# Moving a routing table's one-hot rows to GpSimd, and the first row transposes into the last AV

## Chip, cores and metric

One core of one Trainium2 chip. The time is the device time of one execution in microseconds; the kernel before has a median of 217.82 us over 14 runs (214.29 to 222.69).

## What is computed

Causal attention over 4 batches, 8 heads, 768 positions and a head dimension of 64, in which heads 0, 2 and 6 see the whole past and the others see only 4 sink positions and a window of 64. Its output, as 3072 token rows of 512 elements, goes through a mixture of experts: token n belongs to expert `domain_id[n]`, one of 8.

```python
mask = np.where(retr[0, :, 0, 0, None, None], full_mask, stream_mask)   # per head
a = softmax(np.where(mask, scale * q @ k.T, -1e9))
x = (a @ v).transpose(0, 2, 1, 3).reshape(B * S, H * D)                 # 3072 x 512
for e in range(E):                                                       # 8 experts
    mask = domain_id == e
    h = np.maximum(x[mask] @ w1[e], 0.0)                                 # 512 -> 1024
    out[mask] = h @ w2[e]                                                # 1024 -> 512
```

## The kernel before

The program is written in one order by hand, and each engine works through its own instructions in that order. It has three parts.

**Attention.** 16 pairs of heads, four to a batch: (0, 2), (6, 7), (1, 3), (4, 5). A loop over n = 0 to 16 does the scores of pair n and the AV product of pair n - 1. In pass n, `hooks(n)` issues on the SP queue the loads of q, k and v of pair n + 4, and on GpSimd the casts to fp16: q and k of pair n + 2 (`cast_qk`, L155), v of pair n + 1 (`cast_v`, L175). The fp32 q and k tiles have 3 buffers each, the fp32 v tiles 4, the fp16 q and k tiles 2. So the load of q for pair n + 3 needs pair n's cast, and the cast of pair n + 2 needs pair n's transposes. TensorE transposes q and k (L302), VectorE or ScalarE copies them out of PSUM (L311), TensorE makes the scores (L338, with mask matmuls L321), ScalarE the exponentials (L349), TensorE the AV product (L391), and VectorE normalises (L403, L404) into `xb`. `store_x(b)` (L417) writes a batch's rows to a table `x_tok` in DRAM.

A pass has one to three steps, by the pair's kind: 3 for (0, 2), 2 for (6, 7), 1 for the other two. Behind step x of pass n stand the pieces of the routing that a table names for (n, x).

**Routing.** `routing_items` makes, from the domain ids, the slot of each token: one-hot of the experts (`one_hot`), counts ahead of each partition by three small matmuls (`ranks`), a running count (`scan`), the own rank (`own`), the slot number `dst` (`place`, `place2`), its low 7 bits `lof` and its high part `hif` (`split`). Then the slot table is turned round by a matmul: for each of the 24 token columns, a one-hot row of the low part over 128 (`low`, L577, tiles `ohl`) and of the high part over 28 (`high`, L555; `high2` L563 and `high3` L571 multiply it by the column and by the partition number, tile `ohh`). `rows` multiplies them by 24 matmuls (L588) and starts the conversion on VectorE, `rows2` and `rows3` finish it: `out_i`, and the row numbers `map_i` (all batches) and `map_e` (the first three batches only). `flags` sets a flag for a slow path that is not taken here. All arithmetic of the routing is VectorE's.

**MoE.** Experts are handled in pairs, in groups of 128 slots. `load_w` (L194 for w1, L201 for w2) loads and converts weights; `load_xe` (L661) gathers rows of `x_tok` by `map_e` or `map_i` by indirect DMAs. All these are issued on GpSimd's queue. Of pairs 0 and 1, groups 0, 1, 3 and 4 hold tokens of the first three batches in their first 256 slots of an expert ("early" gathers, issued from `hooks(14)`); groups 2, 6 and 5 ("late") need batch 3 as well and follow `store_x(3)`. `x_transpose` (L683) turns rows, VectorE copies them (L696, L690), `layer1` (L711, L718) and `layer2` (L761, L775) follow, and the results leave by indirect DMAs (L727).

In the last pass, n = 16, there are no scores. TensorE is given dummy matmuls on a zero tile (`keep_warm`, L842): four ahead of the last AV and eight behind it, and after these the first row transposes.

```python
if n == NPAIR:
    av0 = [lambda: keep_warm(4, "exp")] + av0
    av1 = av1 + [lambda: keep_warm(8, "last"), lambda: x_transpose(0, 0, 1, wide=True)]
```

Of the kernel before, what the change touches and what calls it, by code (L numbers as in the profile page):

```python
# [9 lines left out]
FP16 = mybir.dt.float16  # L10
FP32 = mybir.dt.float32
# [10 lines left out]
def kernel(  # L22
# [125 lines left out]
            )  # L148
            q32_t[nm, n] = t

    def cast_qk(n, engs=None):
        for x, nm in enumerate("qk"):
            t = tpool.tile([P, NSO, 2, D], FP16, tag=f"{nm}16", name=f"{nm}_{n}")
            eng = engs[x] if engs else nc.gpsimd
            eng.tensor_copy(  # L155
                out=t[:].rearrange("p t h d -> p h t d"), in_=q32_t[nm, n][:]
            )
            qk_t[nm, n] = t
# [32 lines left out]
    def load_w(e, which):  # L191
        if which == 1:
            t = wpool.tile([P, 2, 2, F], FP16, tag="w1", name=f"w1_{e}")
            nc.gpsimd.dma_start(  # L194
                out=t[:].rearrange("p c r f -> p c (r f)"),
                in_=moe_w1[e].rearrange("(c p r) f -> p c (r f)", p=P, r=2),
            )
        else:
            tag = "w2" if e < 6 else "w1"
            t = wpool.tile([P, 2, 4, DM], FP16, tag=tag, name=f"w2_{e}")  # L200
            nc.gpsimd.dma_start(  # L201
                out=t[:].rearrange("p c r d -> p c (r d)"),
                in_=moe_w2[e].rearrange("(c p r) d -> p c (r d)", p=P, r=4),
            )
        w_t[e, which] = t
# [210 lines left out]
    def store_x(b):  # L416
        nc.sync.dma_start(  # L417
            out=x_d[1 + b * S : 1 + (b + 1) * S, :].rearrange("(p t) d -> p t d", p=P), in_=xb[b][:]
        )


    def routing_items():
        V = nc.vector
        R = {}

        def tile_(shape, dtype, name):
            R[name] = rpool.tile(shape, dtype, name=name)
            return R[name]
# [13 lines left out]
        dest_i = tile_([P, NT], I32, "dest_i")  # L442
        lo = tile_([P, NT], I32, "lo")
        hi = tile_([P, NT], I32, "hi")
        lof = tile_([P, NT], FP16, "lof")
        hif = tile_([P, NT], FP32, "hif")
        fl = tile_([1, 2], FP32, "fl")
        ohl = [
# [55 lines left out]
        def place():  # L504
            V.tensor_scalar(out=odd[:], in0=dom32, scalar1=1, scalar2=None, op0=ALU.bitwise_and)
            V.scalar_tensor_tensor(
                out=dst[:], in0=dom32, scalar=float(CAP), in1=rank[:], op0=ALU.mult, op1=ALU.add
            )
            V.scalar_tensor_tensor(
                out=dst[:], in0=odd[:], scalar=float(MAIN - CAP), in1=dst[:],  # L510
                op0=ALU.mult, op1=ALU.add,
            )
            V.tensor_scalar(
                out=ta[:], in0=odd[:], scalar1=float(HALF - MAIN), scalar2=float(MAIN),
                op0=ALU.mult, op1=ALU.add,
            )
            V.scalar_tensor_tensor(
                out=ta[:], in0=rank[:], scalar=float(MAIN + 1), in1=ta[:],
                op0=ALU.is_ge, op1=ALU.mult,
            )  # L520
# [39 lines left out]
            )  # L560

        def high2():
            V.tensor_tensor(  # L563
                out=ohh[:, :, 1, :],
                in0=ohh[:, :, 0, :],
                in1=c32[:, CF_T : CF_T + NT].unsqueeze(2).to_broadcast([P, NT, NHI]),
                op=ALU.mult,
            )

        def high3():  # L570
            V.tensor_scalar(  # L571
                out=ohh[:, :, 0, :], in0=ohh[:, :, 0, :], scalar1=c32[:, CF_P : CF_P + 1],
                scalar2=None, op0=ALU.mult,
            )

        def low(t):
            V.tensor_tensor(  # L577
                out=ohl[t // 12][:, t % 12 : t % 12 + 4, :],
                in0=c16[:, C_IO : C_IO + P].unsqueeze(1).to_broadcast([P, 4, P]),
                in1=lof[:, t : t + 4].unsqueeze(2).to_broadcast([P, 4, P]),  # L580
                op=ALU.is_equal,
            )

        def rows():
            t_ = ps_s.tile([P, 1024], FP32, tag="sp", name="map_ps")
# [31 lines left out]
        def rows3():  # L617
# [19 lines left out]

        lows = [lambda t=t: low(t) for t in range(0, NT, 4)]
        return {
            (1, 0): (one_hot,), (1, 1): (ranks,), (2, 0): (scan,), (3, 0): (own,),  # L640
            (4, 0): (place,), (4, 1): (place2,), (4, 2): (split,), (5, 0): (high,),
            (6, 0): (high2,), (7, 0): (high3,), (8, 0): lows[0:1], (8, 1): lows[1:2],
            (8, 2): lows[2:3], (9, 0): lows[3:4], (9, 1): lows[4:5], (10, 0): lows[5:6],
            (11, 0): (rows,), (12, 0): (rows2,), (12, 1): (rows3,), (12, 2): (flags,),
        }

    xe_t, xT_t, hT_t = {}, {}, {}
# [24 lines left out]
    def x_transpose(pr, *gs, wide=False):  # L672
        for e in (2 * pr, 2 * pr + 1):
            if e not in xT_t:
                xT_t[e] = mpool.tile([P, 4, CAP], FP16, tag="xT", bufs=4, name=f"xT_{e}")
        if wide:
            ps = ps_s.tile([P, 4, 4, P], FP16, tag="sp", name=f"xtp_{pr}_{gs[0]}")
        else:
            ps = ps_b.tile([P, 2, 4, P], FP16, tag="b", name=f"xtp_{pr}_{gs[0]}")
        for x, g in enumerate(gs):  # L680
            for c in range(4):
                c1, r = divmod(c, 2)
                nc.tensor.transpose(  # L683
                    out=ps[:, x, c, :],
                    in_=xe_of(pr, g)[:, c1 * 256 + r : (c1 + 1) * 256 : 2],
                    identity=id_sb,
                )
        if gs[0] == 6:
            for i in range(2):
                nc.vector.tensor_copy(  # L690
                    out=xT_t[2 * pr + i][:, :, MAIN:CAP],
                    in_=ps[:, 0, :, i * HALF : (i + 1) * HALF],
                )
        else:
            e, o, n = 2 * pr + gs[0] // 3, (gs[0] % 3) * P, len(gs)
            nc.vector.tensor_copy(  # L696
                out=xT_t[e][:, :, o : o + n * P].rearrange("p c (g k) -> p c g k", g=n),
                in_=ps[:, 0:n].rearrange("p g c k -> p c g k"),
            )
# [110 lines left out]
    def hooks(n):  # L810
        b, pi = divmod(n, 4)
        if n == 4:
            for r in range(VR):
                load_vs(r, 1)
        if n + 4 < NPAIR:
            load_qk(n + 4)
            load_v((n + 4) // 4, (n + 4) % 4)
        if n + 2 < NPAIR:
            cast_qk(n + 2)
        if n == 14:  # L820
            for g in (0, 1):
                load_xe(0, g, 3)
        if n + 1 < NPAIR:
            cast_v((n + 1) // 4, (n + 1) % 4)
        if n == 13:
            load_w(0, 1)
        if n == 14:
            load_w(1, 1)
            for g in (3, 4):
                load_xe(0, g, 3)  # L830
            load_w(2, 1)
            for g in (0, 1):
                load_xe(1, g, 3)
            load_w(3, 1)
            for g in (3, 4):
                load_xe(1, g, 3)

    def keep_warm(m, tag):
        pool, tag_, cols = (ps_b, "b", 512) if tag in (0, 1) else (ps_s, "sp", 1024)
        ps = pool.tile([P, cols], FP32, tag=tag_, name=f"warm_{tag}")  # L840
        for _ in range(m):
            nc.tensor.matmul(  # L842
                out=ps[:, 0:DM], lhsT=zrow[:, 0:P], rhs=zrow[:], start=True, stop=True
            )
# [8 lines left out]
    for n in range(NPAIR + 1):  # L853
        if n < NPAIR:
            hooks(n)
        R = len(plans[n % 4]) // 2 if n < NPAIR else 1
        av0, av1 = av_items(n - 1) if n >= 1 else ([], [])
        tr = []
        if n == NPAIR:
            av0 = [lambda: keep_warm(4, "exp")] + av0  # L860
            av1 = av1 + [lambda: keep_warm(8, "last"), lambda: x_transpose(0, 0, 1, wide=True)]
        elif n + 1 < NPAIR:
            q_evac = nc.scalar.copy if R == 1 else nc.vector.tensor_copy
            tr = [lambda: transposes(n + 1, q_evac, R == 1)]
        if R == 1:
            run(tr)
        if n == 0:
            av0 = [lambda: keep_warm(3, 0)]
        steps = {1: [av0 + av1], 2: [tr, av0 + av1], 3: [av0 + av1, tr, []]}[R]
        for x, step in enumerate(steps):  # L870
            if n < NPAIR:
                scores(n, (2 * x, 2 * x + 1))
            run(step)
            if x == 0 and n % 4 == 0 and 0 < n < NPAIR:
                store_x(n // 4 - 1)
            for fn in route.get((n, x), ()):
                fn()
    store_x(B - 1)
    load_w(0, 2)
    for g in (2, 6, 5):  # L880
        load_xe(0, g)
    for g in (2, 6, 5):
        load_xe(1, g)
    load_w(1, 2)
    for g in range(4):
        load_xe(2, g)
# [159 lines left out]
```

## Time and profile before

| what | value |
|---|---|
| median of 14 runs | 217.82 us |
| the profiled execution's own time | 218.66 us |
| its span, first to last instruction | 216.9 us |
| TensorE busy | 187.6 us (86%) |
| VectorE busy | 95.2 us (44%) |
| ScalarE busy | 90.0 us (41%) |
| GpSimd busy | 118.9 us (55%) |
| granted TensorE clock, mean | 0.936 |
| chain that ended last, largest parts | TensorE 70%, DMA 11%, GpSimd 6%, VectorE 5% |

The profile names each instruction by its line in the kernel (L155 is line 155). PE is TensorE's matmuls, PEld its weight loads, DVE VectorE, ACT ScalarE, POOL GpSimd, SP the queue that loads q, k and v. A timeline row has the start and the duration in us, and in brackets the idle time of the engine before it with what ended that. The chain of waits is followed back from the last instruction, at each step to what released it. Busy shares are means over the whole span; what a piece of work costs is read from its own stretch.

### The profile page before, as it was taken

The page shows a single profiled execution, that of the slowest core. Times are in us where ns is not written, and L with a number is a line of the kernel's source. Part 1 is how long each engine was busy: PE and PEld are TensorE (multiplying, and loading weights), DVE is VectorE, ACT ScalarE, POOL GpSimd, SP SyncE. Part 2 cuts the span into 40 slices and gives each one's busy share as a digit, 9 for nine tenths or more (in the row PEclk, how much of TensorE's full clock was granted, in tenths as well). Part 3 has the DMA queues.
Part 4 walks back from the last instruction along what each step waited for, and adds up shares of the span by engine and source line. Part 5 has one row for each costly group of instructions (what it writes and reads, how often), then busy time and mean ns, then how long its engine had stood idle before and what let it go on. Part 6 is the DMA issues. An engine that isn't in the chain of part 4 may idle for free.

```text
span 216.9 us, 5471 instructions
## 1 busy us (share of the span) xinstructions
PE 187.6 (86%) x2295; PEld 124.5 (57%) x2295; DVE 95.2 (44%) x200; ACT 90.0 (41%) x115; POOL 118.9 (55%) x154
## 2 busy tenths in 40 slices
PE   7687795999899798889957899999999999999920
PEld 2345663787587366569955895555554555444510
DVE  4337689867998965331201204440045200444310
ACT  2474585658887755306523571006600165000000
POOL 7815778644757667700578712657837600550670
PEclk9799999579999969789996999999999999999985
DMA  6999999999999899999949999997899999961241
GB/s 194 284 286 303 303 278 272 342 324 299 314 328 274 277 165 216 238 235 275 217 119 179 259 193 214 257 165 246 146 186 259 239 217 243 259 214 51 105 158 65
DMA packets 44448, 49.87 MB, mean 230 GB/s; under 512 B 28799, under 2 KB 37248, under 8 KB 44418
## 3 DMA queue, kind: packets, MB, share of 16 engines
q0 software_dynamic: 9472, 26.80, 55.2%
q1 hardware_dynamic: 34802, 22.60, 37.5%
q8 instruction: 20, 0.33, 0.6%
q10 hardware_dynamic: 144, 0.07, 0.2%
q14 instruction: 10, 0.08, 0.1%
HBM read 56.83 MB, written 10.49 MB: 310 GB/s over the span
## 4 chain that ended last, share of the span: by engine, by line
PE 70%; DMA 11%; POOL 6%; DVE 5%; issue 3%; ACT 2%; SPq 1%; POOLq 1%
PE h L711 23%; PE o L761 18%; DMA k<-in_k_dram 11%; PE av L391 8%; PE sp L338 5%; PE xtp L683 4%; PE o2h L775 3%; POOL k L155 2%; PE sp L321 2%; PE tp L302 1%; POOL out_dram L727 1%; DVE kT L311 1%; POOL ve L175 1%; ACT eT L349 1%; SPq L145 1%
## 5 line engine op out<-in xcount | busy, mean ns | idle before, releaser
L349 ACT ACTIVATE eT<-sp 128x1024 f16<-128x1024 f32 (+2 forms) x56 | 50.2, 953 | 19.4 <-PE sp L338 19.4
L718 ACT ACTIVATE hT<-h 128x512 f16<-128x512 f32 (+2 forms) x48 | 31.8, 668 | 61.2 <-PE h L711 58.6
L711 PE MATMUL h<-xT,w 128*128 128x256 f16 (+2 forms) x384 | 51.7, 293 | 5.3 <-issue 1.9
L727 POOL DMA_INDIRECT out_dram<-oute,out_i x27 | 27.2, 1006 | 42.6 <-DVE oute L725 31.0
L711 PEld LDWEIGHTS <-w 128*128 128x128 f16 x384 | 39.2, 114 | 16.3 <-issue 4.5
L761 PE MATMUL o<-w,hT 128*128 128x512 f16 x184 | 41.9, 379 | 0.0
L725 DVE COPY oute<-o 128x512 f32<-128x512 f32 x23 | 15.9, 692 | 51.6 <-PE o L761 48.9
L761 PEld LDWEIGHTS <-hT 128*128 128x128 f16 x184 | 17.5, 98 | 19.8 <-issue 0.8
L338 PE MATMUL sp<-qT,kT 64*64 64x128 f16 (+8 forms) x468 | 22.6, 255 | 5.1 <-DVE kT L311 3.7
L661 POOL DMA_INDIRECT xe<-x_tok,map_i x16 | 16.3, 1018 | 16.6 <-SPq L950 12.1
L391 PEld LDWEIGHTS <-eT 128*128 128x128 f16 (+2 forms) x672 | 21.8, 104 | 6.2 <-issue 3.2
L391 PE MATMUL av<-ve,eT 128*128 128x65 f16 (+2 forms) x572 | 23.6, 199 | 1.0 <-POOL ve L175 0.7
L155 POOL CAST q<-q 128x768 f16<-128x768 f32 x15 | 12.9, 857 | 18.5 <-DMA q<-in_q_dram 12.3
L696 DVE COPY xT<-xtp 128x1024 f16<-128x1024 f16 (+1 forms) x16 | 8.9, 553 | 26.4 <-PE xtp L683 22.9
L338 PEld LDWEIGHTS <-kT 64*64 64x64 f16 (+2 forms) x468 | 11.7, 105 | 12.5 <-issue 4.4
L404 DVE TENSOR_TENSOR xb<-av,rcp 128x384 f16<-128x384 f32 x32 | 17.8, 558 | 1.1
L321 PE MATMUL sp<-c16s 128*128 128x128 f16 (+2 forms) x152 | 15.7, 297 | 2.2 <-ACT eT L349 1.9
L175 POOL CAST ve<-v 128x384 f16<-128x384 f32 x32 | 17.2, 565 | 0.0
L155 POOL CAST k<-k 128x768 f16<-128x768 f32 x15 | 12.8, 854 | 5.8 <-DMA k<-in_k_dram 5.1
L321 PEld LDWEIGHTS <-c16s 128*128 128x128 f16 (+1 forms) x152 | 7.7, 107 | 6.8 <-issue 5.8
L403 DVE RECIPROCAL rcp<-av 128x6 f32<-128x6 f32 x32 | 6.1, 192 | 11.5 <-PE av L391 11.5
L661 POOL DMA_INDIRECT xe<-x_tok,map_e x8 | 8.3, 1043 | 4.7 <-DVE fl L549 1.9
(96 smaller groups left out, 169.9 us busy)
## 6 DMA issues: line engine op xcount, KB each, us to landing
w<-in_moe_w_dram POOLq DMA_DIRECT2D x16, 1024.0 KB
q<-in_q_dram SPq DMA_DIRECT2D x16, 384.0 KB, 6.3
k<-in_k_dram SPq DMA_DIRECT2D x16, 384.0 KB, 5.9
v<-in_v_dram SPq DMA_DIRECT2D x32, 192.0 KB, 5.8
x_tok<-xb SPq DMA_DIRECT2D x4, 768.0 KB, 6.4
out_dram<-oute,out_i POOLq DMA_INDIRECT x27
c16s<-c SPq DMA_DIRECT2D x1, 320.5 KB, 6.2
xe<-x_tok,map_i POOLq DMA_INDIRECT x16
```

The lines of the kernel that those rows point to most:

```text
L155: eng.tensor_copy(out=t[:].rearrange("p t h d -> p h t d"), in_=q32_t[nm, n][:])
L175: nc.gpsimd.tensor_copy(out=ve_t[b][:, :, h, 0:D], in_=v_t[b, pi][:, hh])
L321: nc.tensor.matmul(out=sp[o, c : c + w], lhsT=c16[rows, C_ID + rows.start : C_ID + rows.stop], rhs=c16[rows, col : col + w], start=(c // 5 ...
L338: nc.tensor.matmul(out=sp[o : o + m, c : c + w], lhsT=kT[n][rows, k0 : k0 + m], rhs=qT[n][rows, i0 : i0 + w], start=False, stop=True, skip ...
L349: nc.scalar.activation(out=eT[n, r // 3][:, r % 3, c0:c1], in_=sp[:, c0:c1], func=AF.Exp, scale=scale)
L391: nc.tensor.matmul(out=ps[m0 : m0 + m, it, :], lhsT=eT[n, r // 3][rows, r % 3, c : c + m], rhs=rhs, start=(cell["n"] == 1), stop=(cell["n" ...
L404: nc.vector.tensor_tensor(out=xb[b][:, :, h * D : (h + 1) * D], in0=ps[:, :, 0:D], in1=rcp[:].unsqueeze(2).to_broadcast([P, NSO, D]), op=A ...
L661: nc.gpsimd.indirect_dma_start(out=xe_of(pr, g), out_offset=None, in_=x_d[0 : 1 + nb * S, :], in_offset=bass.IndirectOffsetOnAxis(ap=(map_ ...
L711: nc.tensor.matmul(out=pv[:, a, c0:c1], lhsT=w_t[e, 1][:, c // 2, c % 2, fc * 512 + fr : (fc + 1) * 512 : 4], rhs=xT_t[e][:, c, c0:c1], st ...
L718: nc.scalar.activation(out=hT_t[e][:, 2 * f2 : 2 * f2 + 2, c0:c1], in_=pv[:, :, c0:c1], func=AF.Relu)
L727: inst = nc.gpsimd.indirect_dma_start(out=out, out_offset=bass.IndirectOffsetOnAxis(ap=out_i[:, s : s + 1], axis=0), in_=o[:], in_offset=None,
L761: nc.tensor.matmul(out=ps[:], lhsT=hT_t[e][:, f, g * P : (g + 1) * P], rhs=w_t[e, 2][:, f // 4, f % 4, :], start=(f == 0), stop=(f == 7),)
```

## The change

It has five parts.

1. The 24 one-hot rows of the low part go from six VectorE instructions of 4 x 128 elements to 24 GpSimd instructions of 128 (a comparison with a scalar that is read per partition; `lof` becomes fp32 for that). The products `high2` and `high3` go to GpSimd as well; `high` stays on VectorE.
2. The table that places the routing's pieces is rewritten: the count, scan and rank pieces come one step or so earlier, the rest of `place` (now `place1`), `place2` and `split` stand together behind step (4, 2), the one-hot rows at (5, 0), (5, 1), (8, 0) to (8, 2) and (9, 0), `rows` at (12, 0) in place of (11, 0), and `rows2`, `rows3` at (12, 1) and (12, 2).
3. The load of expert 0's w1, which stood behind the v cast of pair 14, is issued between the q and k casts of pair 15.
4. Both groups of dummy matmuls in the last pass go, and the first row transposes stand in the middle of the last AV's first half.
5. Behind the last store, the six late gathers are issued ahead of the load of expert 0's w2.

In the order of GpSimd's instructions the compares come in three groups: eight between the v cast of pair 6 and the q cast of pair 8, twelve between the v cast of pair 9 and the q cast of pair 11, four and then `high2` between the v cast of pair 10 and the q cast of pair 12; `high3` follows the v cast of pair 11. Ahead of the first compare the built program has one instruction more than before, a reload of GpSimd's instruction library.

```diff
-    def cast_qk(n, engs=None):
+    def cast_qk(n, engs=None, between=None):
         for x, nm in enumerate("qk"):
+            if x and between:
+                between()
...
-        lof = tile_([P, NT], FP16, "lof")
+        lof = tile_([P, NT], FP32, "lof")
...
                 out=dst[:], in0=odd[:], scalar=float(MAIN - CAP), in1=dst[:],
                 op0=ALU.mult, op1=ALU.add,
             )
+
+        def place1():
...
         def high2():
-            V.tensor_tensor(
+            G.tensor_tensor(
...
         def high3():
-            V.tensor_scalar(
+            G.tensor_scalar(
...
         def low(t):
-            V.tensor_tensor(
-                out=ohl[t // 12][:, t % 12 : t % 12 + 4, :],
-                in0=c16[:, C_IO : C_IO + P].unsqueeze(1).to_broadcast([P, 4, P]),
-                in1=lof[:, t : t + 4].unsqueeze(2).to_broadcast([P, 4, P]),
-                op=ALU.is_equal,
-            )
+            for u in range(t, t + 4):
+                G.tensor_scalar(
+                    out=ohl[u // 12][:, u % 12, :], in0=c16[:, C_IO : C_IO + P],
+                    scalar1=lof[:, u : u + 1], scalar2=None, op0=ALU.is_equal,
+                )
...
-            (1, 0): (one_hot,), (1, 1): (ranks,), (2, 0): (scan,), (3, 0): (own,),
-            (4, 0): (place,), (4, 1): (place2,), (4, 2): (split,), (5, 0): (high,),
-            (6, 0): (high2,), (7, 0): (high3,), (8, 0): lows[0:1], (8, 1): lows[1:2],
-            (8, 2): lows[2:3], (9, 0): lows[3:4], (9, 1): lows[4:5], (10, 0): lows[5:6],
-            (11, 0): (rows,), (12, 0): (rows2,), (12, 1): (rows3,), (12, 2): (flags,),
+            (0, 2): (one_hot,), (1, 0): (ranks,), (1, 1): (scan,), (2, 0): (own,),
+            (3, 0): (place,), (4, 2): (place1, place2, split), (5, 0): lows[0:1],
+            (5, 1): lows[1:2], (8, 0): lows[2:3], (8, 1): lows[3:4], (8, 2): (lows[4], high),
+            (9, 0): lows[5:6], (9, 1): (high2,), (10, 0): (high3,),
+            (12, 0): (rows,), (12, 1): (rows2,), (12, 2): (rows3,), (13, 1): (flags,),
...
-            cast_qk(n + 2)
+            cast_qk(n + 2, between=lambda: load_w(0, 1) if n == 13 else None)
...
-        if n == 13:
-            load_w(0, 1)
...
         if n == NPAIR:
-            av0 = [lambda: keep_warm(4, "exp")] + av0
-            av1 = av1 + [lambda: keep_warm(8, "last"), lambda: x_transpose(0, 0, 1, wide=True)]
+            k = len(av0) // 2
+            av0 = av0[:k] + [lambda: x_transpose(0, 0, 1, wide=True)] + av0[k:]
...
     store_x(B - 1)
+    for pr in range(2):
+        for g in (2, 6, 5):
+            load_xe(pr, g)
     load_w(0, 2)
-    for g in (2, 6, 5):
-        load_xe(0, g)
-    for g in (2, 6, 5):
-        load_xe(1, g)
     load_w(1, 2)
```

More of the change, by code (lines that the diff above doesn't have):

```diff
@@ L422, in routing_items @@
     def routing_items():
-        V = nc.vector
+        V, G = nc.vector, nc.gpsimd
         R = {}
```

## The prediction

> **What bounds the kernel now.** I read the page's busy shares and slices first, then the timelines of GpSimd and TensorE, and last the chain of waits.
>
> ```profile
> PE 187.6 (86%) x2295; PEld 124.5 (57%) x2295; DVE 95.2 (44%) x200; ACT 90.0 (41%) x115; POOL 118.9 (55%) x154
> ...
> PE   7687795999899798889957899999999999999920
> ...
> POOL 7815778644757667700578712657837600550670
> ...
> DMA  6999999999999899999949999997899999961241
> ```
>
> No engine is full over the span; TensorE is nearest (187.6 of 216.9 us). The slices are 5.4 us wide. Up to slice 17 (93 us) this is attention, from there the MoE, where TensorE works without a break from 126 to 206 us. So the MoE is a block of fixed length behind the attention stage, and what counts is when TensorE reaches it. GpSimd looks half idle in slices 7 to 13. That is the time the change spends, so I looked at what the idle time is.
>
> ```profile
> 37.75 1.00 POOL L175 CAST ve<-v 128x384 f16<-128x384 f32 x2
> 40.10 0.83 POOL L155 CAST q<-q 128x768 f16<-128x768 f32 x1 [1.35 <-DMA q<-in_q_dram]
> 41.28 1.19 POOL L155 CAST k<-k 128x768 f16<-128x768 f32 x1 [0.34 <-DMA k<-in_k_dram]
> ...
> 58.90 0.83 POOL L155 CAST q<-q 128x768 f16<-128x768 f32 x1 [0.45 <-PE tpq L302]
> 59.67 0.83 POOL L155 CAST k<-k 128x768 f16<-128x768 f32 x1
> ```
>
> GpSimd timeline: start, duration, and in brackets the idle time before. After the v casts of pair 6 (37.75 to 38.75) GpSimd pauses before the casts of q8 (40.10) and k8, and so on; k12 is cast by 60.50. From 38.75 to the last cast of k15 (73.94) the bracketed pauses sum to 13.45 us. Each is a wait for a load or for TensorE to free a cast buffer.
>
> ```profile
> 47.78 0.51 PE L302 MATMUL tp<-c16s,q 128*128 128x128 f16 x6
> ...
> 64.65 0.51 PE L302 MATMUL tp<-c16s,q 128*128 128x128 f16 x6
> ...
> 76.23 1.33 PE L338 MATMUL sp<-qT,kT 64*64 64x512 f16 x24 [1.22 <-DVE kT L311]
> ```
>
> TensorE timeline: the transposes of pair 8 start at 47.78, those of pair 12 at 64.65. So the casts lead their users by some 4 to 6 us: a cast may slip by that and TensorE doesn't see it. The last line is a place where TensorE waits 1.22 us on VectorE, for k of pair 13.
>
> ```profile
> 89.99 1.79 PE warm_exp L842 x4
> 91.78 1.91 PE av L391 x42
> 93.69 1.83 PE warm_last L842 x8
> 95.52 0.46 PE xtp L683 x8
> 96.00 0.70 DVE xT L696
> ...
> 96.75 1.91 PE h L711 x16
> ```
>
> Chain of waits: between the AV of pair 14 (ends 89.99) and the first layer-1 matmul (96.75) lie 6.76 us, of which 1.79 and 1.83 are dummy matmuls and 0.46 + 0.75 the first row transpose and its copy.
>
> [...] In the instruction order of the changed kernel a library reload stands on GpSimd's queue right ahead of the first one-hot row; the kernel before has none[...]. [...] the granted clock was 0.57 over 76 to 80 us, behind the 1.22 us wait and its neighbours. [...] 58.90 to 59.67 is 0.77 us for a 768-element cast where its row says 0.83.
>
> **The change part by part.**
>
> *One-hot rows to GpSimd.* VectorE loses six 512-element compares (0.68 to 0.86 us each, some 4.8 us) and two products over 672 elements (0.85, 0.39). TensorE was waiting for none of them in 53 to 65 us (busy 11.29 of 12.00), so this alone is worth nothing. GpSimd gains:
> - the reload, L. [...] I take 9.
> - 24 compares of 128 elements, c each. From casts of 768 (0.77 apart) and 384 elements (0.44) a straight line gives 0.11 + 0.86 ns an element, so 0.22 for 128. [...] I take 0.55, near the upper end because even a 48-element memset records 314 ns.
> - the product on two tensors, h: [...]
>
> GpSimd is in order, so I lay its queue out again from 38.75. Pair by pair: q and k casts 2 x 0.77 = 1.54, v casts 0.95, one memset 0.07. Eight compares stand between the casts of v6 and q8, twelve between v9 and q11, four and h between v10 and q12.
> - k8 done: 38.75 + L + 8c + 1.54 = 38.75 + 9 + 4.4 + 1.54 = 53.7. Pair 8's transposes wanted it at 47.78: TensorE waits 5.9 us, and a halved clock after such a wait costs up to half of 3.4, 1.7.
> - k12 done: 38.75 + L + 24c + h + 5 x 1.54 + 4 x 0.95 + 0.07 = 50.3 + 9 + 13.2 + 1.6 = 74.1, wanted at 64.65: 9.5 us late. This is the larger lag and contains the first (47.78's 5.9 + 1.7 bring TensorE to pair 12 at 72.3, where it waits again). k11 (67.8 against 61.40 + 7.6) adds nothing.
> - After k12 the queue catches up: h3 (1.8) and pair 13 are done at 78.4, wanted at 71.72 + 9.5 = 81.2. That cover of 2.8 us hides the second product; without it, it would cost its excess.
>
> So the attention stage ends D = L + 24c + h - 14.3 = 9.5 us later. Behind the compares wait the casts; behind the casts the SP queue, because the load of q11 needs q8's buffer: it is issued at about 52 and not 47.6. Loads land some 5 to 6 us after issue (median 5.9 to 6.3), q11 before 59, its cast stands behind the twelve compares anyway: nothing more.
>
> *Slot numbers behind evacuations, table a step later.* The routing instructions are the same in number. Scan and rank come a step earlier, in gaps of VectorE: nothing. The table (24 small matmuls, 1.07 us) moves behind pair 11's AV, and VectorE has 1.46 us of table work (69.12 to 70.58 before) ahead of pair 13's q/k copies in place of 2.28 (72.18 to 74.46): 0.8 of the 1.22 us wait goes. The row map comes about 1.2 us later against TensorE, and the early gathers with it; the last of them had landed at 104.6 in the trace's DMA records for a use at 106.53, so at D = 9.5 with the gain below they are still in time (about 1 us is left).
>
> *First w1 load between q15 and k15.* 0.76 us on GpSimd ahead of k15's cast, which is wanted 7.7 us after it ends: hidden.
>
> *Row transposes inside the last AV, no dummies.* Both dummy groups go. AV of pair 15 then waits for the second exp (88.48 + 1.94 = 90.41, so 0.45 us), takes 1.91 as before, the transposes 0.46; the 0.69 us copy lies beside the second half of AV. 2.83 for 6.76: gain 3.9. If the AV runs at full clock 0.6 more; if the halved clock moves into layer 1 instead, 1.7 less; if the rows haven't landed, the AV waits in its middle.
>
> *Late gathers sooner.* Six gathers go ahead of w2 of expert 0. Before, the first was issued at 104.72 and used at 115.67, without a wait: the order is worth nothing to TensorE. The w2 load is issued about 8 us (6 x 1.30) after the store lands and is used in layer 2 some 20 us later: nothing.
>
> Sum: +9.5 - 0.8 - 3.9 = +4.8 us. On the profiled execution's own 218.66 that is 223.5; this one lay 0.8 above the median of 217.82, so the forecast is 222.6.
>
> **Rivals.** What differs by over 1% (2.2 us) is about what a measurement of this kernel can tell from no change.
> 1. GpSimd's pauses swallow it (faster). With L = 6, c = 0.30, h = 1.1, D is 0 by the formula and 0.9 at pair 8. For it: 13.45 us of pauses. Then the end gain shows, but only to where the early rows bind: 106.53 - 104.6 + 0.7 for the earlier w1 = 2.6 us. 0.9 - 0.8 - 2.6 = -2.5: 215.3. It decides when L + 24c + h falls below 17.
> 2. Even: L = 6.5, c = 0.45, h = 1.6 give D = 4.6 against a gain of 4.7: 217.7. From 17 to 21.
> 3. Worse: L = 11, c = 0.65, h = 2.2 give D = 14.5, and a gain of 4.7 less 1.7 for a cold start of layer 1: +11.5, 229.3.[...]
> 4. The change doesn't do what it says: the reload isn't paid[...]. Then L = 0 and D < 2, which ends as rival 1.
>
> **How the numbers follow.** Forecast case (sum above 21) 0.56, rival 3 0.14, rival 2 0.13, rivals 1 and 4 together 0.17. The forecast case's own range is 220 to 227. The range reaches down to rival 1 and up to near rival 3: 215.5 to 228.5. Slower by over 1% is the forecast case and rival 3: 0.70; within 1% 0.13; faster 0.17.
>
> **What would show it.** Right: a hole of 6 to 11 us on GpSimd after pair 6's casts, compares 0.3 to 0.65 apart, TensorE waiting before pair 8's and pair 12's transposes on GpSimd's casts, no wait before pair 13's scores, and 3 us from pair 14's AV to layer 1. Wrong: no hole, or k12's cast done before TensorE gets to it; then the forecast is too slow. If the AV of pair 15 waits for gathered rows, the gain of 3.9 fails.

## The result, and the profile after

The changed kernel takes 223.78 us (median of 10 runs, 219.51 to 225.58) where the kernel before takes 218.06 on the same chip: a ratio of 1.0355, 95% interval 1.0259 to 1.0452. On a second chip, where both were run again, it was 216.86 against 210.72, ratio 1.0285 (1.023 to 1.0339). It is slower: by 5.7 us between the medians of the first chip, by 7.7 by its ratio, by 6.0 by the ratio of the second. The forecast, 222.6, is close; most of the terms that make it up are not, as the profile shows. Its profiled execution took 225.44 us (span 223.7), near the top of the range, so what is special to it is told apart below. Ratios leave disturbed runs out and medians don't, so in what follows a median can lie above what its ratio says.

From the page of the changed kernel, the busy shares and the slices:

```profile
PE 188.6 (84%) x2283; PEld 126.1 (56%) x2283; DVE 91.5 (41%) x192; ACT 89.6 (40%) x115; POOL 134.0 (60%) x180
...
PE   7658988898688859869987999999959999999930
...
POOL 7716596989999938820178827515874530351571
...
DMA  6999999999999595999237999999899999971232
```

GpSimd has 15.1 us more work, VectorE 3.7 less. GpSimd's slices 7 to 13 (each 5.6 us wide) stand at 8 and 9 where they were at 4 to 7. TensorE has new holes in the attention (slices 10, 14 and 17), and the DMA engines a gap behind it (slices 19 to 21).

The GpSimd timeline of the changed kernel (start, duration, what it does):

```profile
38.21 0.99 POOL L177 CAST ve<-v 128x384 f16<-128x384 f32 x2
39.34 4.70 POOL L582 TENSOR_SCALAR ohl<-c16s,lof 128x128 f16<-128x128 f16 x8
43.99 0.81 POOL L157 CAST q<-q 128x768 f16<-128x768 f32 x1
...
51.66 0.98 POOL L177 CAST ve<-v 128x384 f16<-128x384 f32 x2
52.62 7.61 POOL L582 TENSOR_SCALAR ohl<-c16s,lof 128x128 f16<-128x128 f16 x12
60.18 0.82 POOL L157 CAST q<-q 128x768 f16<-128x768 f32 x1
60.94 0.82 POOL L157 CAST k<-k 128x768 f16<-128x768 f32 x1
61.72 0.96 POOL L177 CAST ve<-v 128x384 f16<-128x384 f32 x2
62.66 2.34 POOL L582 TENSOR_SCALAR ohl<-c16s,lof 128x128 f16<-128x128 f16 x4
64.97 1.31 POOL L567 TENSOR_TENSOR ohh<-ohh,c32s 128x672 f16<-128x672 f16 x1
66.23 0.81 POOL L157 CAST q<-q 128x768 f16<-128x768 f32 x1
67.00 0.82 POOL L157 CAST k<-k 128x768 f16<-128x768 f32 x1
```

The v casts of pair 6 end at 39.20 and the first comparison starts at 39.34. The hole of 6 to 11 us that the forecast rests on isn't there. The 24 comparisons take 14.65 us together, 0.61 each, and `high2` 1.31: within the bounds of the forecast. k12 is cast at 67.82, 7.3 us later than before (60.50).

The TensorE timeline of the changed kernel, from pair 8's transposes on:

```profile
44.97 0.51 PE L304 MATMUL tp<-c16s,q 128*128 128x128 f16 x6
...
61.05 0.51 PE L304 MATMUL tp<-c16s,q 128*128 128x128 f16 x6 [1.96 <-POOL q L157]
...
67.11 0.51 PE L304 MATMUL tp<-c16s,q 128*128 128x128 f16 x6 [0.85 <-DVE xb L406]
67.88 0.51 PE L304 MATMUL tp<-c16s,k 128*128 128x128 f16 x6 [0.26 <-POOL k L157]
...
80.89 1.40 PE L340 MATMUL sp<-qT,kT 64*64 64x512 f16 x24 [2.81 <-DVE kT L313]
```

Pair 8's transposes are in time in this execution, even 2.8 us earlier than before; pair 11's wait 1.96 us for a cast, pair 12's start 67.11 instead of 64.65. And the wait on VectorE at pair 13, which was to shrink from 1.22 us, is 2.81 us. The VectorE timeline of the changed kernel has its reason:

```profile
74.70 0.21 DVE L595 COPY mf<-map_ps 128x56 f32<-128x56 f32 x1
74.94 3.71 DVE L596 TENSOR_SCALAR me<-mf 128x28 f32<-128x28 f32 x1
...
79.02 0.94 DVE L313 COPY qT<-tpq 128x768 f16<-128x768 f16 x1
```

An instruction on 28 elements took 3.71 us, and pair 13's copies stood behind it. The following text calls this a hold: the instruction stands as busy, without a wait ahead of it.

The end of the attention in the changed kernel, TensorE again; the lines answer to those of the kernel before with the two dummy groups:

```profile
94.83 0.91 PE L393 MATMUL av<-ve,eT 64*128 64x65 f16 x30
97.98 0.21 PE L393 MATMUL av<-ve,eT 128*128 128x65 f16 x1 [2.24 <-DVE rcp L405]
...
98.28 1.04 PE L686 MATMUL xtp<-c16s,xe 128*128 128x128 f16 x8
...
100.93 2.96 PE L714 MATMUL h<-xT,w 128*128 128x256 f16 x16
```

From the AV of pair 14 (ends 95.74) to layer 1 are 5.2 us, not 2.83: the last AV waits for VectorE's normalisation, which frees its PSUM buffer. The first 16 matmuls of layer 1 take 2.96 us where they took 1.91; the clock records show half speed from 96.3 to 103.1.

### The profile page after: what moved, and what is told of

The parts are those of the page before. It is cut to its first block, busy times and chain, and to the rows that moved or that the text cites. A ratio compares the mean times of both kernels' runs of the same rounds, so it can differ in the third digit from the quotient of the medians.

```text
span 223.7 us, 5469 instructions
## 1 busy us (share of the span) xinstructions
PE 188.6 (84%) x2283; PEld 126.1 (56%) x2283; DVE 91.5 (41%) x192; ACT 89.6 (40%) x115; POOL 134.0 (60%) x180
## 5 line engine op out<-in xcount | busy, mean ns | idle before, releaser
L393 PE MATMUL av<-ve,eT 128*128 128x65 f16 (+2 forms) x572 | 25.5, 206 | 4.5 <-DVE rcp L405 2.2
L393 PEld LDWEIGHTS <-eT 128*128 128x128 f16 (+2 forms) x672 | 23.8, 108 | 9.7 <-issue 7.0
L664 POOL DMA_INDIRECT xe<-x_tok,map_i x16 | 16.3, 1017 | 18.9 <-SPq L950 14.3
L323 PE MATMUL sp<-c16s 128*128 128x128 f16 (+2 forms) x152 | 16.4, 308 | 2.5 <-ACT eT L351 2.1
L157 POOL CAST q<-q 128x768 f16<-128x768 f32 x15 | 12.4, 825 | 9.4 <-DMA q<-in_q_dram 6.9
L177 POOL CAST ve<-v 128x384 f16<-128x384 f32 x32 | 15.7, 517 | 0.0
L582 POOL TENSOR_SCALAR ohl<-c16s,lof 128x128 f16<-128x128 f16 x24 | 14.6, 624 | 0.1
```

The lines of the kernel that those rows point to most:

```text
L157: eng.tensor_copy(out=t[:].rearrange("p t h d -> p h t d"), in_=q32_t[nm, n][:])
L323: nc.tensor.matmul(out=sp[o, c : c + w], lhsT=c16[rows, C_ID + rows.start : C_ID + rows.stop], rhs=c16[rows, col : col + w], start=(c // 5 ...
L393: nc.tensor.matmul(out=ps[m0 : m0 + m, it, :], lhsT=eT[n, r // 3][rows, r % 3, c : c + m], rhs=rhs, start=(cell["n"] == 1), stop=(cell["n" ...
L664: nc.gpsimd.indirect_dma_start(out=xe_of(pr, g), out_offset=None, in_=x_d[0 : 1 + nb * S, :], in_offset=bass.IndirectOffsetOnAxis(ap=(map_ ...
```

## The experiments

Theory A after this reading: GpSimd's late casts cost most; the order of the late gathers costs something; the earlier transposes give back 1.5 us. Rival B: the wait on VectorE, or the halved clock behind some of the waits, is the larger part. Each group of four kernels shared one chip and the runs of the kernel before on it (medians 210.41, 210.72 and 210.72), so ratios are compared. "Changed" below is the changed kernel.

| run | median us | ratio to before, 95% interval |
|---|---|---|
| rows and products back on VectorE | 211.71 | 1.0037 (1.0006 to 1.0067) |
| w2 first again | 216.12 | 1.027 (1.0222 to 1.0318) |
| dummies back | 221.08 | 1.0314 (1.0249 to 1.038) |
| `me` from PSUM | 217.26 | 1.0263 (1.0211 to 1.0316) |
| changed, again | 216.86 | 1.0285 (1.023 to 1.0339) |
| `me` and `mf` from PSUM | 216.70 | 1.0279 (1.0222 to 1.0336) |
| rows on VectorE and w2 first | 210.69 | 1.0011 (0.9979 to 1.0042) |
| before, with the rows on GpSimd | 217.80 | 1.0345 (1.0285 to 1.0405) |
| before, with the order of late gathers | 215.15 | 1.0049 (1.0012 to 1.0086) |
| before, with the earlier transposes | 211.59 | 1.0024 (0.9989 to 1.0058) |
| half of the rows on VectorE | 213.37 | 1.012 (1.0054 to 1.0185) |
| dummy work in the waits | 219.52 | 1.0353 (1.0274 to 1.0432) |

**Rows back on VectorE**, the rest of the change as it is (`lof` is fp16 again):

```diff
-            for u in range(t, t + 4):
-                G.tensor_scalar(out=ohl[u // 12][:, u % 12, :], ..., scalar1=lof[:, u : u + 1], ...)
+            V.tensor_tensor(out=ohl[t // 12][:, t % 12 : t % 12 + 4, :], ..., op=ALU.is_equal)
...
-            G.tensor_tensor(        # high2, and high3 likewise
+            V.tensor_tensor(
```

> The changed kernel with the 24 compares and both products back on VectorE, all else as changed. Theory A (the compares fill GpSimd's pauses, make the casts of pairs 11 and 12 late, and GpSimd's unbroken run then holds up VectorE's table work, so that TensorE's clock is halved): 4 to 6 us faster than the changed kernel, about 218 to 220, and no wait of TensorE on casts before the transposes of pairs 11 and 12. Rival B (the prediction's sum, where the rows cost 9.5 us and the end gains 3.9): 8 to 9 us faster, about 215.

Almost all of the loss goes: 0.4% is left. By the ratios that is a gain of some 5 us, which is Theory A's range and not rival B's. Part 1 of the change is the loss, and what is left of the change has no gain to set against it.

**w2 of expert 0 first**, rows on GpSimd:

```diff
+    load_w(0, 2)
     for pr in range(2):
         for g in (2, 6, 5):
             load_xe(pr, g)
-    load_w(0, 2)
     load_w(1, 2)
```

> The changed kernel with the load of expert 0's w2 ahead of the late gathers again. Theory A (the load lost its place in a time when the DMA queue had room, and everything behind it on GpSimd's queue comes later): 3 to 4.5 us faster than the changed kernel, about 219.5 to 221, and the wait of 2.9 us before the row transposes of the last expert pair is gone. Rival B (the order is worth nothing, as predicted): same as the changed kernel within 1 us, and the wait stays.

Not that: 1.027 beside the 1.0285 of the changed kernel, no difference that these intervals show. The wait of 2.89 us for late rows that the profile of the changed kernel has is gone from this variant's, as Theory A expected, but the gain that was to come of it is not there.

**Dummies back**, and the transposes behind the last AV:

```diff
-            k = len(av0) // 2
-            av0 = av0[:k] + [lambda: x_transpose(0, 0, 1, wide=True)] + av0[k:]
+            av0 = [lambda: keep_warm(4, "exp")] + av0
+            av1 = av1 + [lambda: keep_warm(8, "last"), lambda: x_transpose(0, 0, 1, wide=True)]
```

> The changed kernel with both groups of dummy matmuls and the row transposes behind the last AV again. Theory A (the dummies stood mostly in a wait for the PSUM buffer and kept the clock up, so their removal gains little): 0 to 2 us slower than the changed kernel, 223.5 to 226. Rival B (the removal gains the predicted 3.9 us): 227 to 228.

1.0314 against 1.0285, with intervals that overlap: of the 3.9 us at most a fraction is seen. The medians lie further apart (221.08 and 216.86), since five of the eight executions took over 220 us here and three of seven there. By the ratio A is within its range and B's 3.9 us are not there.

**`me` from PSUM**, to test the wait on VectorE:

```diff
-                out=me[:], in0=mf[:, 0, :], scalar1=0.0, scalar2=None, op0=ALU.is_equal
+                out=me[:], in0=mp[:, 0, :], scalar1=0.0, scalar2=None, op0=ALU.is_equal
```

> The changed kernel with one edit: the comparison that took 3.71 us on VectorE reads the matmul's result from PSUM and not its copy in SBUF; nothing else differs. Theory A[...]: the instruction takes under 0.5 us, pair 13's q and k copies come some 3 us earlier, TensorE's wait of 2.8 us before the scores of pair 13 falls under 1 us, and the kernel is 2 to 5 us faster. Rival B (VectorE waits for something else, a semaphore or an instruction fetch, which the edit doesn't touch): the instruction still takes over 2 us and the time stays within 1 us.

The time stayed (1.0263). The VectorE timeline of this variant, of an execution of 222.37 us, shows what became of the hold:

```profile
74.92 0.18 DVE L596 TENSOR_SCALAR me<-map_ps 128x28 f32<-128x28 f32 x1
75.04 3.69 DVE L599 SCALAR_TENSOR_TENSOR mf<-mf 128x28 f32<-128x28 f32 x1
78.66 0.94 DVE L313 COPY qT<-tpq 128x768 f16<-128x768 f16 x1
```

`me` went through in 0.18 us while GpSimd was casting (74.85 to 75.81), but the next instruction, which reads two operands from SBUF, took the hold over (3.69 us), and the copies came no sooner (78.66 against 79.02). What makes either instruction stand isn't shown.

**The change again**, on the chip of the following three:

(No edit.)

> The changed kernel itself, on the chip of the four variants. Theory A (rows on GpSimd cost some 6 us, the late w2 of expert 0 some 4, the earlier transposes give back 1.5): its distance to the kernel before is the same here as where it was first measured, 3.5% (2.6 to 4.5), so 217.8 against 210.4. Rival B (most of the cost comes from the clock that is halved in some executions, not from the order of the work): under 2%, and the four variants before it were then no gain over the change.

1.0285, inside the first interval. In this execution `me` took 0.18 us; GpSimd had nothing to do from 75.80 to 79.83, and `me` ran at 77.85. So the 3.7 us hold is not in every execution, and the loss is. Of the profiles, three have it: those of the changed kernel, of "dummies back" (1.58 and 2.08 us, on the two instructions) and of "`me` from PSUM". Pair 8, in time above, waits 2.60 us for its cast here.

**Both instructions from PSUM**:

```diff
-                out=mf[:, 0, :], in0=mf[:, 0, :], scalar=float(NT), in1=mf[:, 1, :],
+                out=mf[:, 0, :], in0=mp[:, 0, :], scalar=float(NT), in1=mf[:, 1, :],
```

> The changed kernel, with both small VectorE instructions that follow the table's evacuation (L596 and L599) reading their first operand from PSUM, so that neither has only SBUF operands or two of them. [...] both take 0.2 us, pair 13's q and k are copied at 75.5 instead of 79.0, TensorE's wait of 2.8 us before pair 13's scores goes, and the attention ends 2 to 3 us sooner; the time falls by 1.5 to 3 us against the changed kernel. Rival (the wait is for something else that ends at 78.7, such as a semaphore of the casts or of a transfer): whatever comes next on VectorE stands until 78.7 as well, as L599 did when only L596 was changed, and nothing is gained.

The VectorE timeline of this variant:

```profile
75.60 0.18 DVE L596 TENSOR_SCALAR me<-map_ps 128x28 f32<-128x28 f32 x1
75.72 0.19 DVE L599 SCALAR_TENSOR_TENSOR mf<-map_ps,mf 128x28 f32<-128x28 f32 x1
76.16 0.96 DVE L313 COPY qT<-tpq 128x768 f16<-128x768 f16 x1 [0.26 <-PE tpq L304]
...
77.90 1.31 DVE L605 TENSOR_SCALAR mf<-me 128x28 f32<-128x28 f32 x1
```

Both take 0.2 us, as expected. But that proves nothing here: GpSimd stood idle from 75.29 to 76.25 in this execution, and in "w2 first" the unedited pair took 0.18 and 0.19 us in such a pause, with L605 at 1.31 as here. The 1.5 to 3 us that were expected did not come: 1.0279. The longest single wait in the profile of the changed kernel has no price that these ratios show; since it is not in every execution, the edit may have had little to remove.

**Rows on VectorE and w2 first**, both edits from above together:

> The changed kernel with the rows and products on VectorE again and expert 0's w2 ahead of the late gathers again: what is left of the change is the earlier slots of the slot numbers, the transposes inside the last AV and the sooner w1. Theory A (the two undone parts are the whole loss): 1 to 2 us under the kernel before, from the 1.5 us at the end of the attention; the experts' part takes 39.9 us as in the kernel before instead of the 40.6 of the variant with the rows alone undone. Rival B (the order of the gathers costs nothing once GpSimd is free in time): the same as the variant with the rows alone undone, 211.7.

1.0011: what the change has besides these two parts is worth nothing either way, and A's 1 to 2 us aren't there. Rival B, no difference from the variant with the rows alone taken back (1.0037), is not excluded, as the intervals overlap. It is the fastest variant of the change and doesn't beat the kernel before.

This variant and "w2 first" differ in the rows alone, and both were profiled in executions without the hold (215.27 us, the shortest of "w2 first", median 216.12; and 210.62, median 210.69; on two chips), so they show best what the rows do. TensorE with the rows on GpSimd (w2 first):

```profile
61.25 0.51 PE L304 MATMUL tp<-c16s,q 128*128 128x128 f16 x6 [1.94 <-POOL q L157]
...
67.28 0.82 PE L304 MATMUL tp<-c16s,q 128*128 128x128 f16 x6 [2.27 <-POOL q L157]
...
76.13 0.51 PE L304 MATMUL tpq<-c16s,q 128*128 128x128 f16 x6
```

and with the rows on VectorE:

```profile
64.29 0.49 PE L304 MATMUL tp<-c16s,q 128*128 128x128 f16 x6 [0.34 <-DVE kT L313]
...
71.57 0.51 PE L304 MATMUL tpq<-c16s,q 128*128 128x128 f16 x6
```

Pair 12 starts 2.99 us later (67.28 against 64.29), pair 13 4.56 later (76.13 against 71.57). The stretch between them has the same work and takes 8.85 instead of 7.28 us, 1.57 more. The table of windows (stretch, length, busy time and instructions of PE, PEld, DVE, ACT and POOL, granted clock, DMA share, GB/s) gives the reason in its granted clock, 0.50 and 1.00; its other columns cover different work in the two. First with the rows on GpSimd, then on VectorE:

```profile
67.30:70.70 3.40, 3.40 (x59) 2.37 (x60) 0.96 (x1) 1.30 (x2) 3.40 (x4) 0.50 1.06 279
```

```profile
67.30:70.70 3.40, 3.10 (x87) 2.40 (x81) 2.09 (x7) 2.48 (x3) 2.07 (x4) 1.00 1.16 282
```

The clock is halved for 3.4 us behind the wait of 2.27 us; half of 3.4, 1.7 us, is about what the stretch lost. Pair 14's AV then ends 4.59 us later, and the end of the span is 4.7 later (213.5 against 208.8). In between the lag changes. The first gather of rows is issued 4.52 us later (81.87 against 77.35), since its row numbers come from the table that TensorE makes in pass 12. TensorE starts layer 1 only 2.24 us later (92.25 against 90.01, where the other variant had lost time in its last AV), but then waits 4.28 us for gathered rows, and its first late transposes are 5.86 behind (115.03 against 109.17). So the lateness reaches the end through the rows as well as through TensorE's own work.

**Before, with the rows on GpSimd**, at the old places (`lof` is fp32):

```diff
-            V.tensor_tensor(out=ohl[t // 12][:, t % 12 : t % 12 + 4, :], ..., op=ALU.is_equal)
+            for u in range(t, t + 4):
+                G.tensor_scalar(out=ohl[u // 12][:, u % 12, :], ..., scalar1=lof[:, u : u + 1], ...)
...
-            V.tensor_tensor(        # high2, and high3 likewise
+            G.tensor_tensor(
```

> The kernel before with the first part of the change alone: the 24 comparisons and two products on GpSimd, at the slots of the kernel before, all else as it was. Theory A: GpSimd's casts from pair 11 on come 3 to 7 us later, TensorE waits for them at pairs 11 to 13; 3 to 6 us slower than before (213.5 to 216.5), with no hole ahead of the first comparison. Rival B (GpSimd's pauses of 13 us in the attention take the 15 us): within 1 us of before. The prediction's step (a reload of some 9 us ahead of the first comparison): a hole, and 8 us or more slower.

1.0345: part 1 alone costs as much as the whole change. Its GpSimd timeline, around the first of the moved instructions:

```profile
42.25 0.96 POOL L175 CAST ve<-v 128x384 f16<-128x384 f32 x2
43.27 1.31 POOL L563 TENSOR_TENSOR ohh<-ohh,c32s 128x672 f16<-128x672 f16 x1
```

No hole here either: 0.06 us. TensorE then waits 3.30 us for q12's cast. Rival B, and the forecast's reload, both fall; A's direction holds, with a loss of 7.3 us (3.45% of 210; 6.0 to 8.5 by the interval), 1.3 over its range.

**Before, with the order of the late gathers**:

```diff
+    for pr in range(2):
+        for g in (2, 6, 5):
+            load_xe(pr, g)
     load_w(0, 2)
-    for g in (2, 6, 5):
-        load_xe(0, g)
-    for g in (2, 6, 5):
-        load_xe(1, g)
```

> The kernel before with its order of late transfers alone changed: the late gathers of the first two expert pairs ahead of expert 0's w2, all else as it was. Theory A (the w2 transfer fits beside the gathers' waiting when it is first, and queues with two others when it is last; the pair of variants with the rows on VectorE differ by 0.26% in this way): 0 to 1 us slower. Rival B (the trace of the changed kernel, where the experts' part took 5 us longer, shows the order's own price): 4 us slower or more. The prediction's step: nothing.

1.0049: some 1.0 us, at A's upper end. The median says more: 12 of the 22 executions took 214.85 to 219.60 us, where 2 of 43 of the kernel before on this chip took as long. The profiled one (214.85) waits 1.81 and 2.09 us for late rows, where the profiles of the kernel before and of "w2 first" have no such wait. With this order and the rows on VectorE ("rows back on VectorE") only 2 of 22 took so long. Whether the order brings such executions on is not shown.

**Before, with the earlier transposes**:

```diff
-            av0 = [lambda: keep_warm(4, "exp")] + av0
-            av1 = av1 + [lambda: keep_warm(8, "last"), lambda: x_transpose(0, 0, 1, wide=True)]
+            k = len(av0) // 2
+            av0 = av0[:k] + [lambda: x_transpose(0, 0, 1, wide=True)] + av0[k:]
```

> The kernel before with the end of the attention alone changed: the twelve dummy products away and the first row transposes in the middle of the last AV. The prediction's step: 3.9 us faster. Theory A (the last AV then waits for the PSUM buffer that VectorE's normalisation frees, and the products of layer 1 that follow wait for the rows of the gathers anyway): 0 to 1.5 us faster. Rival B (without the dummies the clock falls where they stood): 1 us slower or more.

1.0024, and its interval has no room for 3.9 us. One line of its GpSimd timeline, and then its TensorE timeline:

```profile
60.02 0.83 POOL L155 CAST k<-k 128x768 f16<-128x768 f32 x1 [0.30 <-DMA k<-in_k_dram]
```

```profile
60.91 0.51 PE L302 MATMUL tp<-c16s,k 128*128 128x128 f16 x6
...
83.80 0.91 PE L391 MATMUL av<-ve,eT 64*128 64x65 f16 x30
85.53 0.19 PE L391 MATMUL av<-ve,eT 128*128 128x65 f16 x1 [0.82 <-DVE rcp L403]
...
87.83 1.94 PE L711 MATMUL h<-xT,w 128*128 128x256 f16 x16
91.06 0.74 PE L683 MATMUL xtp<-c16s,xe 128*128 128x128 f16 x8 [1.30 <-DMA xe<-x_tok,map_e]
91.63 3.66 PE L711 MATMUL h<-xT,w 128*128 128x256 f16 x32
98.96 0.74 PE L683 MATMUL xtp<-c16s,xe 128*128 128x128 f16 x8 [3.67 <-DMA xe<-x_tok,map_e]
```

The end of the attention is as short as forecast: 3.12 us from the end of pair 14's AV (84.71) to layer 1, where 2.83 were worked out. But two of the early gathers' rows aren't there yet, and TensorE waits 1.30 and 3.67 us for them. The gain turns into a wait 3 and 11 us later.

**Half of the rows on VectorE**: comparisons for the first 12 columns on GpSimd, the other 12 on VectorE.

```diff
+            if t < 12:
                 for u in range(t, t + 4):
                     G.tensor_scalar(...)
+            else:
+                V.tensor_tensor(...)
```

> The changed kernel with the last 12 of its 24 comparisons on VectorE again, in three products over four tiles as in the kernel before; the other 12 and both products stay on GpSimd. Theory A (GpSimd has some 14 us of slack before a cast is late: 12 comparisons of 0.62 and products of 3.3 us are 10.7 us and fit): TensorE waits for no cast at pairs 11 and 12, and the time is that of the variant with all rows on VectorE, 211.7 against 210.7 (0.5% over before, within 0.5 of it). Rival B (every comparison on GpSimd costs its share[...]): half of the loss stays, 213.5 to 214.5.

1.012, between the two, and not within 0.5 us of A's 211.7. B's half of the loss lies within the interval, but no trace shows that each comparison pays a share. A was right that pairs 11 and 12 wait for no cast, and wrong about the slack further up. GpSimd and then TensorE of this variant:

```profile
37.17 0.83 POOL L157 CAST q<-q 128x768 f16<-128x768 f32 x1 [2.10 <-DMA q<-in_q_dram]
...
40.20 4.67 POOL L583 TENSOR_SCALAR ohl<-c16s,lof 128x128 f16<-128x128 f16 x8
44.83 0.81 POOL L157 CAST q<-q 128x768 f16<-128x768 f32 x1
```

```profile
45.70 0.82 PE L304 MATMUL tp<-c16s,q 128*128 128x128 f16 x6 [3.21 <-POOL q L157]
```

The first eight comparisons fall behind a late load in this execution, and pair 8 pays for it: 3.21 us, and the clock at 0.50 from 45.7 to 49.0. So pair 8's place, which the forecast named, has little slack, even without a reload. The same eight comparisons cost pair 8 a wait of 0.74 us in "w2 first", 1.91 in "`me` and `mf` from PSUM" and 2.60 in "changed, again"; that it makes up the 1.2% of this variant is likely, not shown.

**Dummy work in the waits**:

```diff
+        for _ in range({11: 36, 12: 12}.get(n, 0)):
+            nc.tensor.transpose(out=halves[0][:, NSO, :], in_=id_sb, identity=id_sb)
         for x, nm in enumerate("qk"):
             for t in range(NSO):
```

> The changed kernel with dummy transposes ahead of pair 11's (36) and pair 12's (12), in columns of the PSUM tile that nothing reads, so that TensorE works where it waits for GpSimd's casts. Theory C (the halved clock after these waits, 7 to 14 us long in the traces, is a good part of the loss): no halved stretch between 58 and 80 us, and 1.5 to 3.5 us off the changed kernel: 213.5 to 215.5. Rival D (the loss is the casts' lateness itself, the clock follows elsewhere): the casts of pairs 11 and 12 end at 61.9 and 67.9 as before, and the time stays within 0.7 of 216.9.

Neither gain nor a clear loss (1.0353, overlapping 1.0285); D's 0.7 us around 216.9 isn't met either. Its TensorE timeline:

```profile
58.82 2.17 PE L303 MATMUL tp<-c16s 128*128 128x128 f16 x36
61.50 0.51 PE L306 MATMUL tp<-c16s,q 128*128 128x128 f16 x6 [0.51 <-POOL q L157]
...
67.54 0.51 PE L306 MATMUL tp<-c16s,q 128*128 128x128 f16 x6 [1.50 <-POOL q L157]
```

Pair 11's wait is filled and the clock stays full (1.00 over 58 to 69 us). Behind the unfilled 1.94 us in "w2 first" it was full as well (1.00 over 63.9 to 67.3). Pair 12's twelve were too few: 1.50 us remain, and the clock is at 0.50 from 69.1 to 79.3. What the halved clock costs over many executions, apart from the casts' lateness, is left open; theory C's gain wasn't seen.

## Why the prediction came out right, and where its steps were wrong

The sum was +9.5 - 0.8 - 3.9 = +4.8 us; measured are +5.7 between the medians of the first chip, +7.7 by its ratio and +6.0 by the ratio on the second (2.85% of 210). The direction and the path, casts late behind the comparisons, are right; the largest term of the path is not. Term by term:

- **L, the reload, 9 us: wrong, 0.1.** The 9 us were the author's estimate, like the 6 and 11 around them; no trace stood behind it. The trace of the change has 0.14 us between the last cast and the first comparison, that of the rows alone 0.06. The measurement decides: this reload cost nothing visible; why, no run shows. "No hole" was also the sign by which the forecast was to be too slow; the hole is missing and the kernel is as slow all the same.
- **c and h: right as figures.** 0.61 against 0.55, 1.31 against 1.6, both inside their bounds (0.30 to 0.65, 1.1 to 2.2); `high3` 1.97 against 1.8. The figures and their bounds were the author's estimates. Only the straight line through the casts (0.22 us for 128 elements) and the memset's 0.31 us come from a trace, and the comparisons take more than either.
- **The slack, 14.3 us: too large, by 2 to 5.** With the measured prices of "w2 first", 14.25 for the comparisons and 1.27 for `high2` from start to start, and L = 0, the formula gives 1.2 us of lateness for k12. It was done at 68.00, 3.35 after 64.65. The sum began at 38.75 and left GpSimd no pause from there on; in that trace pair 6's casts end at 39.51 (0.76 later), and pauses of 0.93 and 0.31 for pair 10's casts remain. Of the 13.45 us of pauses, those that wait for loads or for buffers that TensorE frees are not all free to be filled. And the sum took its deadlines from one execution. In the trace of the earlier transposes alone, whose attention is that of the kernel before up to the last pass, pair 8's transposes start at 43.30 and not at 47.78, and k12's cast (60.02 to 60.85, shown above) ends just ahead of its user (60.91): the lead of 4 to 6 us isn't there. Pair 6's casts end at 39.58 and pair 12's first transposes start at 60.51 in it, so the prediction's own sum gives 9.4 us of slack, and the measured prices some 6 of lateness, an estimate from these figures. Not all of that need reach the end: this trace takes 10.42 us from there to pair 13, where 7.28 were seen with the rows on VectorE.
- **The halved clock: right in size, not complete in place.** 1.7 at pair 8 was worked out, half of 3.4 us. The trace of the kernel before has stretches of that length (0.51 over 76.3 to 79.7 us, 0.53 over 90.2 to 93.6), but also 0.50 over 38.8 to 45.5, and the changed kernel stands at 0.50 over 79.2 to 89.4: 1.7 is not an upper bound. The half of the rows has it at pair 8 (0.50 from 45.7 to 49.0). Behind pair 12 it stood in the sum at nothing; 1.57 were lost there.
- **-0.8 at pair 13: no gain shown.** The wait of 1.22 us is 2.81 in the profile of the changed kernel and absent in that of "w2 first"; but it is absent with the old table too, in the trace of the earlier transposes alone.
- **-3.9 at the end: wrong as time.** The stretch itself became 3.12 us long with the earlier transposes alone, but the time didn't fall. The step counted the gathered rows as in time, with about 1 us left at D = 9.5. Rival 1 named this bound; here the wait for the rows took the whole gain. In the full change the last AV also waits for its PSUM buffer (0.82 us in most of the traces, 2.24 in the profiled one), which the sum lacked.
- **Late gathers, nothing: about right by the ratios.** 1.0 us of loss when made alone, 0.5 between the two variants with the rows on VectorE, whose intervals overlap. The long executions of the order made alone leave a larger price open.

So the forecast's number was met by luck, by errors that cancel: 9 us too much in one term, and 2 to 5 of slack, the halved clock and 3.9 of gain too favourable in others. The rows alone give, in the pair of traces, 3.0 us at pair 12 and 1.6 of halved clock, 4.6 together at the end of pair 14's AV. That the span ends 4.7 later is near to it in part by chance, since the lag moves between 2.24 and 5.86 on the way. Rival 4, no reload and therefore a faster kernel, was right that no reload is seen and wrong in its end, since it took the slack and the gain of 3.9 for granted.

## What to carry to other kernels

An engine that casts for the bottleneck engine isn't half idle because its busy row says so: lay out each pause with what ends it, and count as free only those that no load and no buffer dictates. Read the deadlines of the users from more than one execution, since a slack is a difference of two times that both move. Shortening a stretch pays only if what comes next is there; look up when the data for the following two steps land before a gain is booked. And the longest wait of one profiled execution is a hypothesis: the edit that removes it tells whether it was worth its length.

## What the runs showed of the hardware that was not expected

A VectorE instruction on 28 elements stood for 3.71 us (74.94 to 78.65) in the profile of the changed kernel, while GpSimd worked without a pause: back-to-back casts from 72.27 to 76.50, a transfer's issue of 0.86 us at 76.45, and casts again from 77.32 to 79.05. When it was given a PSUM operand, it took 0.18 us beside a running cast, and the next one, with two SBUF operands, stood for 3.69 (75.04 to 78.73) over the same row of casts and issue. Where GpSimd paused 0.87 us, in "w2 first", the same two instructions went through at 0.18 and 0.19 (at 76.23 and 76.44). So, at the same 0.18 and 0.19, did the unedited pair in "changed, again" and with half of the rows on VectorE; in "dummies back" they stood for 1.58 and 2.08. The hold stands where GpSimd casts without a pause and is absent where it pauses 0.87 us; what holds VectorE isn't shown. With a PSUM operand in both, the only trace has a pause of GpSimd at that place, so it doesn't tell.
